# Attention's loads spread between products, w_out three slices ahead, conversions into buffers of their own

## The chip, the cores and the metric

One core of a Trainium2 chip runs the whole program. The metric is device time in microseconds (us) of one execution; lower is better. The engines are PE (TensorE, matmuls), DVE (VectorE), ACT (ScalarE), POOL (GpSimd) and SP (SyncE, which here does nothing but start DMA transfers). Each engine works through its own list of instructions in program order. A DMA is started by an instruction on an engine's queue: SPq is SP's, ACTq is ScalarE's.

## What is computed

```python
# attention in chunks of 64 along the sequence (q, k, v: 8 x 8 x 576 x 64)
scores = scale * np.matmul(q_c, k_c.transpose(0, 1, 2, 4, 3))
scores = scores - np.max(scores, axis=-1, keepdims=True)
attn = np.exp(scores)
attn = attn / (np.sum(attn, axis=-1, keepdims=True) + 1e-09)
out = np.matmul(attn, v_c)
x = np.ascontiguousarray(attn_out.transpose(0, 2, 1, 3)).reshape(B * S, H * D)   # 4608 x 512
# phase 0, d_ff 1536
x = ((x @ w_a) * (x @ w_b)) @ w_out
# phase 1, d_ff 1024
h = ((x @ w1) * (x @ w2)) @ w3
return h @ w_out2
```

## The kernel before

The 4608 tokens are nine blocks of 512. A block's attention comes in four **units** (two heads each); a unit loads q and k (`load1`) and v (`load2`) from memory with many small DMAs, turns them (`turn`), and goes on with `scores`, `soft1`, `soft2`, `flip`, `apply`, `put`. These pieces are laid by a planner, `Track`, between the matmul products of the block before: at every `point()` between products it emits pieces in step with their planned costs. `load1` and `load2` start all DMAs of their unit in a row on SP's queue: in blocks of full-length runs 16 for q and k, 12 for v.

Values are split into a high and a low part (`split`: a cast on ACT, a subtraction on POOL or DVE), and a product is three passes of matmuls over these parts.

A phase begins with **plain steps** (block 0 and part of block 1, `plain_step`), during which the weights are converted; then come **Strassen blocks** of two token blocks each (`strassen_step`, 12 steps in phase 0, 8 in phase 1; seven products P1 to P7 per step), and last the **lone block** (the ninth, at half width). The second factor's product, g times w_out, is done slice by slice (`Second`, four parts of three matmuls) one step behind. For the other token block of a pair it is done in a **burst** between two Strassen blocks: `burst` runs all slices in a row, 12 or 8, after the first of which the pending slice of the last step is finished. For each slice it needs `wo` (512 KB of w_out, loaded on SP's queue, four buffers, two slices ahead) and `gh`, `gl` (the two parts of g, made by `g_parts` on ACT and POOL, three buffers). During a burst the next block's attention begins: `attention_begins` starts the loads of its first two units before the first slice. During the steps of the first Strassen block of a phase, sums of weights (`su`, loaded two steps ahead) are formed on DVE and `w` tiles are loaded on SP's queue when a product has set their buffer free (`load_part`).

The weights arrive as float32 and are converted by `Conv`, driven by `Pump`: `load` (a DMA of 512 KB into a raw tile `cv`), `s1` (DVE, ACT), `s2` (three operations on DVE, then one addition on POOL which writes the result over a third of the raw tile), and a `sink` that casts the result on ACT and subtracts on DVE or POOL one job later. In the lone block of phase 0 this is done for w_out2 (jobs `o2`) and w3 (`w3`, two per row block; each is turned by PE in `turn_w3` two jobs later, and `fuse` multiplies it by w_out2), with three raw buffers (`G2`, `xo1`, `xo2`). The result stays in the raw tile until its last reader is done; only then can the next load go into that buffer.

`tick()` stands ahead of every product and every part of a slice; it sends off waiting stores on ACT's queue. On SP's queue everything goes out in program order, and an instruction that waits for a buffer holds all behind it.

## Time and profile before

| | |
|---|---|
| median of 3 runs | 1890.5 us (1886.52 to 1900.22) |
| the profiled execution | 1885.44 us, span 1883.6 us |
| mean granted TensorE clock in it | 0.937 of full speed |
| busy: PE | 1621.7 us, 86% of the span |
| busy: DVE, ACT, POOL | 882.9, 558.7, 442.2 us |
| DMA | 385.45 MB, 291704 packets |

Busy time of PE is that of pipelined matmuls, whose ends are modelled; a busy PE is not PE at its peak. The share is an average over stages that have different limits, so the stages are looked at one by one. In the timeline, each row gives the start, the duration, the engine, the line of the kernel, the operation with output and inputs, a count, and in brackets how long the engine had been idle and what ended that.

### The profile page before, as it was taken

The page shows a single profiled execution, that of the slowest core. Times are in us where ns is not written, and L with a number is a line of the kernel's source. Part 1 is how long each engine was busy: PE and PEld are TensorE (multiplying, and loading weights), DVE is VectorE, ACT ScalarE, POOL GpSimd, SP SyncE. Part 2 cuts the span into 40 slices and gives each one's busy share as a digit, 9 for nine tenths or more (in the row PEclk, how much of TensorE's full clock was granted, in tenths as well). Part 3 has the DMA queues.
Part 4 walks back from the last instruction along what each step waited for, and adds up shares of the span by engine and source line. Part 5 has one row for each costly group of instructions (what it writes and reads, how often), then busy time and mean ns, then how long its engine had stood idle before and what let it go on. Part 6 is the DMA issues. An engine that isn't in the chain of part 4 may idle for free.

```text
span 1883.6 us, 24887 instructions
## 1 busy us (share of the span) xinstructions
PE 1621.7 (86%) x9232; PEld 1308.6 (69%) x9232; DVE 882.9 (47%) x1484; ACT 558.7 (30%) x1009; POOL 442.2 (23%) x354
## 2 busy tenths in 40 slices
PE   5679994999876999699998577789989989989998
PEld 3567783777655787477877466677867867868787
DVE  5667662576652555445324443346554442242231
ACT  4444442322232222232223221223233232142232
POOL 1323331211121121221223221123221221222222
PEclk7879997999998999899999789899999999999999
DMA  7657754666755666666566565558647756656675
GB/s 194 226 169 238 248 196 110 215 198 217 234 160 175 189 190 212 178 214 196 179 193 220 186 223 189 168 200 317 234 149 270 260 178 219 212 184 205 192 271 176
DMA packets 291704, 385.45 MB, mean 205 GB/s; under 512 B 174848, under 2 KB 195328, under 8 KB 291584
## 3 DMA queue, kind: packets, MB, share of 16 engines
q1 hardware_dynamic: 259328, 299.97, 51.4%
q10 hardware_dynamic: 32256, 83.90, 11.5%
q8 instruction: 73, 1.20, 0.3%
q14 instruction: 47, 0.39, 0.1%
HBM read 301.99 MB, written 81.79 MB: 204 GB/s over the span
## 4 chain that ended last, share of the span: by engine, by line
PE 65%; DVE 9%; DMA 8%; SPq 6%; issue 5%; ACT 4%; POOL 3%; ACTq 1%; POOLq 0%; DVEq 0%
PE P L735 32%; PE acc L764 19%; PE pb L721 5%; PE pa L721 4%; PE wf L966 3%; SPq L278 2%; DMA cv_o<-in_moe_w_out_dram 2%; SPq L300 2%; DMA cv_w<-in_moe_w_dram 2%; DVE xP L539 1%; DVE xP L225 1%; PE x L371 1%; PE s L321 1%; DMA wo<-dwo 1%; DVE c L823 1%
## 5 line engine op out<-in xcount | busy, mean ns | idle before, releaser
L735 PE MATMUL P<-xP,w 128*128 128x512 f32 (+1 forms) x3360 | 741.1, 374 | 72.1 <-DVE c L823 30.7
L735 PEld LDWEIGHTS P<-xP,w 128*128 128x128 f32 x3360 | 592.0, 195 | 194.3 <-DVE c L823 40.1
L823 DVE TENSOR_TENSOR c<-P,c 128x512 f32<-128x512 f32 (+1 forms) x240 | 148.7, 622 | 338.6 <-PE P L735 330.7
L851 POOL TENSOR_TENSOR G<-c,c 128x512 f32<-128x512 f32 x60 | 77.9, 1299 | 514.5 <-DVE c L823 514.5
L820 ACT COPY c<-P 128x512 f32<-128x512 f32 (+1 forms) x240 | 127.1, 532 | 224.7 <-PE P L735 220.4
L764 PE MATMUL acc<-gh,wo 128*128 128x512 f32 x480 | 175.2, 403 | 0.0
L224 ACT CAST gh<-c 128x512 fp32r<-128x512 f32 x60 | 37.3, 621 | 326.1 <-DVE c L850 311.4
L721 PE MATMUL pa<-xq,w 128*128 128x512 f32 x480 | 123.0, 407 | 1.9 <-DVE w L624 1.9
L721 PE MATMUL pb<-xq,w 128*128 128x512 f32 x480 | 123.7, 409 | 0.0
L225 POOL TENSOR_TENSOR gl<-c,gh 128x512 fp32r<-128x512 f32 x60 | 77.9, 1298 | 159.9 <-ACT gh L224 159.9
L764 PE MATMUL acc<-wo,gh 128*128 128x512 f32 x320 | 111.1, 390 | 0.5 <-ACT gh L224 0.5
L721 PEld LDWEIGHTS pa<-xq,w 128*128 128x128 f32 x480 | 92.5, 196 | 22.8 <-DVE w L624 2.3
L721 PEld LDWEIGHTS pb<-xq,w 128*128 128x128 f32 x480 | 93.4, 197 | 20.5 <-DVE w L624 0.2
L764 PEld LDWEIGHTS acc<-gh,wo 128*128 128x128 f32 x480 | 92.9, 194 | 19.8
L225 DVE TENSOR_TENSOR xP<-xP,xP 128x512 fp32r<-128x512 f32 (+1 forms) x64 | 52.4, 819 | 105.0 <-ACT xP L224 105.0
L850 DVE TENSOR_TENSOR c<-P,c 128x512 f32<-128x512 f32 x60 | 41.5, 691 | 119.2 <-PE P L735 119.2
L764 PE MATMUL acc<-gl,wo 128*128 128x512 f32 x240 | 96.0, 400 | 0.0
L179 POOL TENSOR_TENSOR cv<-cv 128x512 f32<-128x512 f32 x40 | 48.3, 1208 | 132.1 <-DVE cv L175 125.4
L225 DVE TENSOR_TENSOR xP<-x,xP 128x512 fp32r<-128x512 f32 (+1 forms) x48 | 45.9, 1002 | 55.1 <-ACT xP L224 55.0
L764 PEld LDWEIGHTS acc<-wo,gh 128*128 128x128 f32 x320 | 60.1, 188 | 13.4 <-ACT gh L224 1.0
L224 ACT CAST xP<-xP 128x512 fp32r<-128x512 f32 (+1 forms) x64 | 36.2, 565 | 103.1 <-DVE xP L539 103.1
L764 PE MATMUL acc<-wo,gl 128*128 128x512 f32 x160 | 62.8, 393 | 0.9 <-POOL gl L225 0.8
(128 smaller groups left out, 2158.8 us busy)
## 6 DMA issues: line engine op xcount, KB each, us to landing
w<-dw SPq DMA_DIRECT2D x200, 512.0 KB, 4.3
wo<-dwo SPq DMA_DIRECT2D x168, 512.0 KB, 4.3
dw<-w ACTq DMA_DIRECT2D x80, 512.0 KB, 3.8
w<-dw SPq DMA_DIRECT2D x80, 256.0 KB, 3.3
d<-cv ACTq DMA_DIRECT2D x40, 256.0 KB, 4.4
su<-d SPq DMA_DIRECT2D x20, 512.0 KB, 5.5
cv_o<-in_moe_w_out_dram SPq DMA_DIRECT2D x19, 512.0 KB, 5.9
x2d<-ev ACTq DMA_DIRECT2D x36, 256.0 KB, 3.0
```

The source lines that it names most:

```text
L179: eng.tensor_tensor(self.w, hi.bitcast(F32), lo, op=ALU.add)
L224: nc.scalar.copy(dst_h, src)
L225: eng_l.tensor_tensor(dst_l, src, dst_h, op=ALU.subtract)
L278: nc.sync.dma_start(tv[g : g + 32, off // 32 : (off + n) // 32, :], src[b, 2 * self.hp + h, s : s + n, 32 * e : 32 * e + 32].rearrange("(t ...
L721: nc.tensor.matmul(ps, w[m][:, kk // 2, wp, kk % 2], xq[kk // 2][:, kk % 2, xp], start=(n == 0), stop=(n == 3 * KM - 1),)
L735: nc.tensor.matmul(ps, w[:, wp, kt], x[:, kt, xp], start=(begins and n == 0), stop=(n == 5), skip_group_check=True,)
L764: nc.tensor.matmul(acc[m], a, b, start=(f == 0 and (wp, gp) == SEQ[0]), stop=(f == NF[ph] - 1 and (wp, gp) == SEQ[-1]),)
L820: nc.scalar.copy(t, src)
L823: add = lambda o, a, b: nc.vector.tensor_tensor(o, a, b, op=ALU.add)
L850: nc.vector.tensor_tensor(g, last, c11, op=ALU.mult)
L851: nc.gpsimd.tensor_tensor(g_place(ph, nm.split("_")[0], f, gplaces), c22, c12, op=ALU.mult)
L966: nc.tensor.matmul(ps, t[:, gp, jj], wo2[jj // 2][:, jj % 2, wp], start=(jj == 0 and (wp, gp) == SEQ[0]), stop=(jj == NF[1] - 1 and (wp, g ...
```

## The change

Five things are changed.

1. Attention's loads are no longer started where `load1` and `load2` stand. `ask` puts them in a list; `tick` sends off two ahead of each product and one ahead of each part of a slice, eight per round in the opening. `settle` sends off what is left of a unit's loads where they are first needed (`turn` for q and k, `sums` for v).
2. In a burst `wo` is asked for three slices ahead instead of two, the first three ahead of the new attention loads' sending.
3. The parts `gh`, `gl` of a burst's first slice are made ahead of the last step that precedes the burst; `gh` and `gl` have four buffers instead of three, `tmp` five instead of six.
4. In the lone block the conversion's last addition writes into a tile of its own (`cw`, four buffers that attention used before), and the next raw tile is asked for right behind every conversion, as far as three ahead.
5. In the opening, three raw weight loads move from SP's queue (and one from the first instruction of ACT's) to ACT's queue, one in each of the first three rounds; the raw loads that stood in later rounds go out from the first plain steps on.

```diff
-        return pool.tile([P, n], F32, tag="tmp", name=name, bufs=6)
+        return pool.tile([P, n], F32, tag="tmp", name=name, bufs=5)
...
+    def ask(to, src):
+        asks["left"].append((to, src))
+        asks["all"] += 1
+
+    def settle(n):
+        while asks["done"] < n and asks["left"]:
+            nc.sync.dma_start(*asks["left"].popleft())
+            asks["done"] += 1
+
-    def tick(every=False):
+    def tick(every=False, loads=0):
+        settle(asks["done"] + loads)
...
             self.w = b.bitcast(F32)
+            if self.out:
+                self.w = pool.tile([P, NT], F32, tag=self.out, name=f"cw_{self.nm}")
             eng.tensor_tensor(self.w, hi.bitcast(F32), lo, op=ALU.add)
...
                         for e in range(2):
                             g = 32 * (2 * h + e)
-                            nc.sync.dma_start(
+                            ask(
...
         def turn(self):
+            settle(self.qk_end)
...
     def product(ps, w, x, begins):
-        tick()
+        tick(loads=2)
...
             self.m += 1
-            tick()
+            tick(loads=1)
...
-        gh = pool.tile([P, NT], F32R, tag="gh", name=f"gh{nm}", bufs=3)
-        gl = pool.tile([P, NT], F32R, tag="gl", name=f"gl{nm}", bufs=3)
+        gh = pool.tile([P, NT], F32R, tag="gh", name=f"gh{nm}", bufs=4)
+        gl = pool.tile([P, NT], F32R, tag="gl", name=f"gl{nm}", bufs=4)
...
-        for f in range(2):
-            ready(f)
+        parts = [ready(ph, j, 0, gplaces) if first is None else first]
+        parts.append(ready(ph, j, 1, gplaces))
+        state["outs"].ahead(3)
...
+            state["outs"].ahead(3)
...
-            return dict(tag=["G2", "xo1", "xo2"][n % 3])
+            return dict(tag=["G2", "xo1", "xo2"][n % 3], out=["qk0", "qk1", "ep0", "ep1"][n % 4])
...
                 pump.run()
-                if kind:
+                while pump.loaded < min(pump.cap, pump.done + 3):
                     pump.load(slot(kind))
...
-        for i in range(4):
+        for i in range(3):
             pump.load(slot("Y"), nc.scalar)
...
-                if t > 1:
-                    pump.load(slot("Y"))
-            tick()
+            if t < 3:
+                pump.load(slot("Y"), nc.scalar)
+            tick(loads=8)
...
+                if f + 1 == n and not single:
+                    state["ready"] = ready(ph, j + 1, 0, gplaces)
...
-                            track.append((1.0, True, lambda ic=turns[n_ - 2]: turned(ic)))
+                            track.append((1.0, True, lambda ic=turns[n_ - 2]: turn_w3(*ic)))
...
-                            track.append(conv_piece(None))
+                            track.append(conv_piece("G"))
```

What the change does to the engines' lists is seen at three places. The first is SP's list at the first burst of phase 0 (`qk` and `v` are attention loads, `wo` the slices of w_out). Before, from the second unit's 28 loads on (the first unit's 28 stand ahead of them):

```order
L278 DMA qk_1_3005<-in_q_dram 32x8x32 x8
L278 DMA qk_1_3005<-in_k_dram 32x8x32 x8
L300 DMA v_1_3022<-in_v_dram 64x2x64 x2
L300 DMA v_1_3022<-in_v_dram 64x64
L305 DMA v_1_3022<-in_v_dram 64x64
L300 DMA v_1_3022<-in_v_dram 64x64
L305 DMA v_1_3022<-in_v_dram 64x64
L300 DMA v_1_3022<-in_v_dram 64x2x64 x4
L659 DMA wo_2_3041<-dwo_2_166 128x1024
L659 DMA wo_3_3100<-dwo_3_167 128x1024
L659 DMA wo_4_3126<-dwo_4_168 128x1024
```

And in the changed kernel:

```order
L680 DMA wo_2_2989<-dwo_2_166 128x1024
L148 DMA qk_0_2981<-in_q_dram 32x8x32 x8
L680 DMA wo_3_3052<-dwo_3_167 128x1024
L148 DMA qk_0_2981<-in_k_dram 32x8x32 x4
L680 DMA wo_4_3082<-dwo_4_168 128x1024
L148 DMA qk_0_2981<-in_k_dram 32x8x32 x4
L680 DMA wo_5_3111<-dwo_5_169 128x1024
L148 DMA v_0_2982<-in_v_dram 64x2x64 x2
L148 DMA v_0_2982<-in_v_dram 64x64 x2
L680 DMA wo_6_3142<-dwo_6_170 128x1024
```

All 56 small loads stood ahead of the third slice's `wo`; now eight stand behind it and four between two slices, for as long as there are any. The second place is POOL's list at the end of the same Strassen block (`gl_3b` are low parts for the burst behind it, `G` and `gl_11` belong to the block's last step). Before:

```order
L851 TENSOR_TENSOR G_2_4672<-c_11_4999,c_11_5032 128x512
L225 TENSOR_TENSOR gl_11_5096<-c_11_5012,gh_11_5095 128x512
L225 TENSOR_TENSOR gl_3b_5156<-G_0_3477,gh_3b_5155 128x512
L225 TENSOR_TENSOR gl_3b_5160<-G_0_3477,gh_3b_5159 128x512
L225 TENSOR_TENSOR gl_3b_5215<-G_0_3477,gh_3b_5214 128x512
```

And in the changed kernel:

```order
L241 TENSOR_TENSOR gl_10_4987<-c_10_4865,gh_10_4986 128x512
L241 TENSOR_TENSOR gl_3b_4991<-G_0_3471,gh_3b_4990 128x512
L872 TENSOR_TENSOR G_2_4671<-c_11_5003,c_11_5036 128x512
L241 TENSOR_TENSOR gl_11_5100<-c_11_5016,gh_11_5099 128x512
L241 TENSOR_TENSOR gl_3b_5108<-G_0_3471,gh_3b_5107 128x512
```

One low part of the burst has moved ahead of the last step's two operations; its cast has done the same on ACT. The third place is POOL's list at the start of the lone block of phase 0 (`cv` are raw tiles, `cw` the new ones). Before:

```order
L179 TENSOR_TENSOR cv_o_0_8987<-cv_o_0_8987 128x512
L179 TENSOR_TENSOR cv_o_1_8989<-cv_o_1_8989 128x512
L179 TENSOR_TENSOR cv_o_2_8991<-cv_o_2_8991 128x512
L847 TENSOR_TENSOR g_0_9089<-c_0_9002,c_0_9050 128x256
L225 TENSOR_TENSOR gl_0_9093<-g_0_9089,gh_0_9092 128x512
```

And in the changed kernel:

```order
L195 TENSOR_TENSOR cw_o_0_9011<-cv_o_0_8989 128x512
L195 TENSOR_TENSOR cw_o_1_9041<-cv_o_1_8991 128x512
L195 TENSOR_TENSOR cw_o_2_9069<-cv_o_2_8993 128x512
L868 TENSOR_TENSOR g_0_9092<-c_0_9002,c_0_9052 128x256
L241 TENSOR_TENSOR gl_0_9096<-g_0_9092,gh_0_9095 128x512
```

Nothing has moved here; the addition's target is another tile, so that it is the raw tile's last reader. On PE's list no instruction has moved anywhere, and on DVE's only the first operation of one conversion, in the first plain step.

## Rows read from the trace of the kernel before

**Rows 1.** The page's head: the span of the profiled execution.

```profile
span 1883.6 us, 24887 instructions
```

**Rows 2.** Stretches: length, busy us of PE, PEld, DVE, ACT, POOL, PEclk, DMA, GB/s.

```profile
291.34:361.40 70.06, 39.59 (x157) 31.55 (x158) 27.48 (x35) 18.26 (x33) 14.64 (x11) 0.78 0.54 161
361.40:542.30 180.90, 165.93 (x1148) 129.71 (x1147) 118.94 (x229) 50.45 (x95) 29.95 (x23) 0.97 0.69 217
542.30:609.39 67.09, 39.08 (x156) 31.53 (x157) 23.55 (x25) 18.76 (x33) 17.99 (x13) 0.80 0.49 143
...
772.47:830.68 58.21, 40.97 (x158) 32.96 (x158) 23.54 (x25) 18.77 (x33) 17.98 (x13) 0.82 0.57 166
...
986.52:1028.20 41.68, 37.94 (x156) 30.50 (x157) 16.79 (x23) 15.79 (x33) 17.19 (x13) 0.96 0.63 201
1028.20:1266.11 237.91, 171.00 (x893) 146.93 (x892) 100.34 (x191) 57.83 (x113) 52.98 (x49) 0.86 0.57 195
...
1379.58:1417.82 38.24, 28.92 (x110) 21.28 (x110) 23.26 (x33) 15.96 (x28) 9.28 (x7) 0.96 0.61 208
...
1515.20:1552.87 37.67, 30.45 (x109) 22.13 (x110) 20.58 (x23) 16.39 (x29) 12.39 (x9) 0.91 0.51 171
...
1650.25:1686.46 36.21, 28.97 (x109) 21.28 (x110) 20.58 (x23) 16.39 (x29) 12.41 (x9) 0.95 0.54 176
```

**Rows 3.** Timeline of PE in the first burst.

```profile
327.99 0.76 PE L764 MATMUL acc<-gh_1b,wo 128*128 128x512 f32 x1 [27.32 <-DMA wo<-dwo]
...
342.96 0.61 PE L764 MATMUL acc<-gh_1b,wo 128*128 128x512 f32 x2
...
343.64 0.61 PE L764 MATMUL acc<-gh_1b,wo 128*128 128x512 f32 x2
```

**Rows 4.** Waits of PE: who waited for whom, us in total, times, longest.

```profile
PE acc L764 <- DMA wo<-dwo: 66.8, 3, 27.3
```

**Rows 5.** Timeline of SP's queue in the first burst.

```profile
291.74 5.24 SPq L278 DMA_DIRECT2D qk<-in_q_dram  x8
...
323.35 20.35 SPq L659 DMA_DIRECT2D wo<-dwo  x9
```

**Rows 6.** Timeline of PE at the start of the second burst.

```profile
543.57 0.51 PE L764 MATMUL acc<-gh_3b,wo 128*128 128x512 f32 x1 [1.27 <-ACT gh_3b L224]
545.68 0.50 PE L764 MATMUL acc<-gl_3b,wo 128*128 128x512 f32 x1 [1.61 <-POOL gl_3b L225]
```

**Rows 7.** Timeline of the lone block: third conversion, and the tenth's addition.

```profile
1037.12 0.33 SPq L159 DMA_DIRECT2D cv_o<-in_moe_w_out_dram  x1
...
1041.22 0.43 DVE L165 TENSOR_SCALAR cv_o<-cv_o 128x512 int32<-128x512 int32 x1 [3.79 <-DMA cv_o<-in_moe_w_out_dram]
...
1043.57 1.36 POOL L179 TENSOR_TENSOR cv_o<-cv_o 128x512 f32<-128x512 f32 x1 [5.58 <-issue]
...
1044.42 4.66 PE L735 MATMUL P<-xP,w 128*128 128x256 f32 x24 [7.52 <-DVE c L823]
...
1092.83 1.04 POOL L179 TENSOR_TENSOR cv_w<-cv_w 128x512 f32<-128x512 f32 x1 [2.16 <-DVE cv_w L175]
```

**Rows 8.** Timeline: a `fuse`, the last w3 addition; chain: products of phase 1's lone block.

```profile
1130.68 5.79 PE L966 MATMUL wf<-wo,w3t 128*128 128x512 f32 x24 [0.69 <-DVE w3t L225]
...
1229.11 1.04 POOL L179 TENSOR_TENSOR cv_w<-cv_w 128x512 f32<-128x512 f32 x1 [2.01 <-PE P L735]
...
1827.79 4.31 PE P L735 x36
```

**Rows 9.** Timeline of the opening: a raw weight load and who waits for it.

```profile
43.76 0.64 SPq L159 DMA_DIRECT2D cv_o<-in_moe_w_out_dram  x1
...
50.84 0.43 DVE L165 TENSOR_SCALAR cv_o<-cv_o 128x512 int32<-128x512 int32 x1 [6.39 <-DMA cv_o<-in_moe_w_out_dram]
```

**Rows 10.** Timeline of the first Strassen block: loads ahead of `su`, and PE.

```profile
445.11 3.90 SPq L278 DMA_DIRECT2D qk<-in_k_dram  x8
...
455.84 1.13 PE L321 MATMUL s<-kT,qT 64*64 64x64 f32 x32 [4.26 <-DVE c L823]
```

More of the change, by code (lines that the diff above doesn't have):

```diff
@@ L137, in store @@
         stores.append([0, to, src])
-    def tick(every=False):
+    asks = {"left": deque(), "all": 0, "done": 0}
+    def ask(to, src):
[7 more added lines that the diff above has]
+        settle(asks["done"] + loads)
         for s in stores:
@@ L154, in load @@
         def load(self, slot, queue=None):
+            self.out = slot.pop("out", None)
             t = pool.tile([P, 3 * NT], I32, name=f"cv_{self.nm}", **slot)
@@ L265, in load1 @@
             self.load_qk()
+            self.qk_end = asks["all"]
         def load2(self):
@@ L269, in load2 @@
             self.load_v()
+            self.v_end = asks["all"]
         def load_qk(self):
@@ L299, in every_other @@
             if whole:
-                nc.sync.dma_start(
+                ask(
                     to[:, c0 : c0 + whole, :],
@@ L304, in every_other @@
             for c in range(whole, cnt):
-                nc.sync.dma_start(to[:, c0 + c, :], hs[s0 + c * P : s0 + c * P + CH, :])
+                ask(to[:, c0 + c, :], hs[s0 + c * P : s0 + c * P + CH, :])
         def turn(self):
+            settle(self.qk_end)
             self.t = [self.work("qT"), self.work("kT")]
@@ L365, in sums @@
         def sums(self, place):
+            settle(self.v_end)
             self.x = self.banks("x")
@@ L410, in load_qk @@
                     for h in range(2):
-                        nc.sync.dma_start(
+                        ask(
                             to[:, :, h],
@@ L423, in load_v @@
                     if off % P == 0 and n % P == 0:
-                        nc.sync.dma_start(
+                        ask(
                             tv[:, off // P : (off + n) // P, h, :],
@@ L436, in turn @@
         def turn(self):
+            settle(self.qk_end)
             self.t = [self.work("qT"), self.work("kT")]
@@ L730, in product @@
     def product(ps, w, x, begins):
-        tick()
+        tick(loads=2)
         n = 0
@@ L880, in plain_step, with ready, burst @@
         point()
-    def burst(ph, j, gplaces, others):
+    def ready(ph, j, f, gplaces):
+        return g_parts(gplaces[f // 4][:, f % 4], f"{ph}_{j}b{f}", nc.gpsimd)
+    def burst(ph, j, gplaces, others, first=None):
         n = NF[ph]
-        sums, parts = [], []
+        sums = []
         track = Track(others, 2 * n // 3)
-        def ready(f):
-            parts.append(g_parts(gplaces[f // 4][:, f % 4], f"{ph}_{j}b{f}", nc.gpsimd))
-        for f in range(2):
-            ready(f)
+        parts = [ready(ph, j, 0, gplaces) if first is None else first]
+        parts.append(ready(ph, j, 1, gplaces))
+        state["outs"].ahead(3)
         for f in range(n):
             if f and f + 2 < n:
-                ready(f + 2)
+                parts.append(ready(ph, j, f + 2, gplaces))
             s = Second(ph, j, f, state["outs"].next(), parts[f], sums, ("rC", "rA", "rB", "rD"))
@@ L902, in burst @@
                 state["pending"].rest()
-                ready(2)
+                parts.append(ready(ph, j, 2, gplaces))
+            state["outs"].ahead(3)
         track.finish()
@@ L1014, in chunk_attention_two_gated_products @@
         U = [First(T, hp, T) for T in range(2) for hp in range(NHP)]
-        for i in range(4):
+        for i in range(3):
             pump.load(slot("Y"), nc.scalar)
-        for u in U[:2]:
+        for u in U[:NHP]:
             u.load1()
             u.load2()
-        for u in U[2:4]:
-            u.load1()
-            u.load2()
+        settle(asks["all"])
         plain = {0: [], 1: []}
@@ L1055, in chunk_attention_two_gated_products @@
                 pump.run()
-                if t > 1:
-                    pump.load(slot("Y"))
-            tick()
+            if t < 3:
+                pump.load(slot("Y"), nc.scalar)
+            tick(loads=8)
         units = unit_list(1)
@@ L1075, in point @@
                 (at or late).point(pe)
+            if n + 1 == len(order):
+                state["ready"] = ready(0, 1, 0, plain[0])
             plain_step(0, 0, T, f, f"0_{T}_{f}", point, plain[0], sums[0], "AC")
@@ L1155, in point @@
                         nxt.point(pe)
+                    if n_ + 1 == len(order):
+                        state["ready"] = ready(1, 1, 0, plain[1])
                     plain_step(1, 0, T, f, f"1_{T}_{f}", point, plain[1], sums[1], "AC" if T else "BD")
@@ L1178, in chunk_attention_two_gated_products @@
                     attention_begins(units)
-                burst(ph, j + 1, places, pieces)
+                burst(ph, j + 1, places, pieces, state.pop("ready", None))
                 steps = NF[ph]
@@ L1192, in chunk_attention_two_gated_products @@
                     track = [conv_piece("G") for i in range(NF[1])]
-                    def turned(ic):
-                        turn_w3(*ic)
-                        pump.load(slot("G"))
                     turns = [(i, c) for i in range(NF[1]) for c in range(2)]
```

## The prediction

> **What bounds it now.** The prediction is made against the profiled execution: 1885.4 us, of which the span is 1883.6 [rows 1]. I first cut the span by stage with the table of stretches, then asked in each slow stage what the Tensor engine (PE) waits for (the list of waits), and last read the timeline there. Where PE is not the bound, two things show. Rows 2 give eight bursts and the lone block. A burst of phase 0 is 13 slices (12 of its own, one pending) of 12 matmuls; three matmuls start 0.68 us after the three before [rows 3], so a slice needs 2.72 us and the burst 35.4 us. It takes 70.1, 67.1, 58.2 and 41.7 us. A burst of phase 1 has 9 slices, 24.5 us; the first three take 38.2, 37.7 and 36.2 us [rows 2]. The lone block takes 237.9 us at a mean granted clock of 0.86. The block of steps between the first two bursts runs at 0.97 [rows 2], so far less is to be had there.
>
> In the bursts the list of waits names one releaser: PE waits for `wo<-dwo`, 66.8 us in 3 times [rows 4]. The timeline shows why: SyncE's queue (SPq) begins with the attention loads of two units at 291.74 and reaches the next `wo` only at 323.35; that is 56 loads in 31.6 us, 0.565 us each [rows 5]. PE restarts at 327.99, 4.6 us after the issue, at 0.76 us for a matmul that otherwise shows 0.39 [rows 3]: the granted clock of this burst is 0.78, so part of it ran at 1.2 GHz instead of 2.4. The fourth burst has no attention loads, and none of this.
>
> **The bursts' loads.** The rows of the order show `wo` first, then 8 loads, then `wo` after every four. Each part of a slice lets one load go, so SPq has 4 x 0.565 and some 0.33 for a large load (as one takes in rows 7), 2.6 us of issuing per slice of 2.72. With three slices ahead, slice 3 is asked for when the pending slice ends and is needed 5.4 us later, against the 4.6 us from issue to use of rows 3 and 5: a slack of about 0.8 us. If a load costs 5.24/8 = 0.66 us, as the first eight do [rows 5], SPq needs 2.97 us per slice and falls 0.25 x 12 = 3 us behind; I take 2 us lost per burst. So bursts 1 to 3 should look like the fourth, 41.7 us.
>
> **The first slice's parts.** Every burst behind a Strassen block starts with PE waiting for the Scalar engine's `gh` (1.27 us) and GpSimd's `gl` (1.61 us) [rows 6]: 2.9 us, six times. After, both stand ahead of the last step in program order and lie under it, one cast and one subtraction in a step whose products keep PE busy; without that cover they cost the same 2.9. With 41.7 - 2.9 + 2 (loads) - 0.8 I take 40 us for bursts 1 to 3 and 38.5 for the fourth. In phase 1 the fourth `gh`/`gl` buffer lets the cast run one slice further ahead of PE; nothing of before shows how much of the remaining excess this takes, bounds being none of it and all. I take about half for the two behind a block: 37.7 and 36.2 become 31 and 30; the first, behind plain steps, goes from 38.2 to 35; the last loses its start, about 3. The gains are 30 + 27 + 18 + 3 + 3 + 7 + 6 + 3 = **97 us** (bounds 60 and 120).
>
> **The lone block.** With three buffers a conversion goes round thus: Vector waits 3.79 us for the load, works from 1041.22, GpSimd's addition ends at 1044.93, the next load starts when the previous job's low part is done [rows 7]. The conversions come 49.3/7 = 7.04 us apart, from the addition at 1043.57 to that at 1092.83, eight additions. The load takes 4.1 us (issued at 1037.12, used at 1041.22), so it was issued 2.9 us after the last conversion began: 2.9 + 4.1 = 7.0, the period. PE's adds stand behind it in Vector's queue, and PE waits 7.52 us at 1044.42. After, the raw buffer is free once the addition has ended, 3.7 us after the start, and the load then issued is wanted two conversions later: 3.7 + 0.1 + 4.1 = 7.9 us for two, 3.9 each, still above the 3.2 us that Vector works on one with its add (1041.22 to PE's restart at 1044.42). I take 4.1: (7.04 - 4.1) x 7 = 20.6 us. Against it stands 2.7: the burst's third slice ahead makes SPq wait one slice longer before it comes to the block's first load.
>
> Then come w3's pairs: from 1092.83 to 1229.11 seven pairs, 19.5 us each [rows 7, 8]. A step of the lone block has 42 products' matmuls, 36 of which take 4.31 us in phase 1, and 12 of w_out [rows 8, 3]: 5.0 + 2.7 = 7.7 us. By its share of the pieces' planned cost a pair stands over 0.96 of a step, and adds `fuse` (24 matmuls at 0.227 = 5.4 us) and two transposes (0.7): 13.5 us for PE. Today a load's wait falls inside, because the raw buffer is held until the transpose two jobs on. After it is not, but the short waits for Vector around `fuse` (0.69 us before it at 1130.68) stay, some more per pair: between 13.5 and 19.5 I take 16 us, 3.5 x 7 = 24. The lone block gives 20.6 - 2.7 + 24 = **42 us** (bounds 15 and 75).
>
> **The rest.** (a) Opening: `cv_o` is issued at 43.76, behind the second block's v loads, and Vector waits 6.39 us for it [rows 9]. After it is asked for on the Scalar engine's queue two rounds earlier: 6 us (2 to 10; the three issues there hold Scalar some 0.6 us each, as SPq's 0.64, 1.9 in all). The Trainium skill's page "DMA: Bandwidth & Descriptors", section "Issuing engines are not separate DMA queues", says another issuing engine saves only issue time. By that the sum would be 5.4 us less; here it is the place in the order that moves. (b) Block 1: 16 q/k loads go out in a row, `su` behind the last 3.90 us of them, and PE stands 4.26 us at 455.84 behind Vector, which waits for `su` [rows 10]; its clock of 0.97 over 181 us [rows 2] is some 5 us more. Spread at most 18 per step (7 products x 2 + 4), they leave `su` in time: 10 us (0 to 15). (c) The plain steps: 4 us (0 to 8). (d) Five instead of six `tmp` buffers: a step takes three or four, so the buffer wanted is one whose last reader stands most of a step earlier in program order, in steps of 7.7 us and more: nothing. That cover gone, a GpSimd operation of 1.36 us [rows 7] would be waited for, at most 1.4 us per step.
>
> Sum: 97 + 42 + 6 + 10 + 4 = 159; 1885.4 - 159 = 1726. The runs' median is 5 us above the profiled execution, their lowest 1 above; I put **1728 us**.
>
> **Rivals.** *The loads choke the queue.* If each attention load holds SPq for twice 0.565 us once they lie between `wo` loads, a slice lasts 4 x 1.13 + 0.33 = 4.85 instead of 2.72 us, 25 us per burst: 1728 + 75 = 1803. For it speaks that 0.66 was seen; against it that a `wo` right behind 56 of them was used after 4.6 us, no backlog. The skill's same page, "Specifications", puts line rate at 512 bytes and up, while q/k rows here are 128 bytes; that is this rival's ground, and no run shows it in a burst so far.
> *The lone block keeps its pace.* If, with the loads away, Vector's and Scalar's queues still pace a conversion at 6.5 us and a pair at 19, its gain is 5: 1728 + 37 = 1765. For it: the waits for `c` adds are many and short; against: the 7.0 is explained by the load alone.
> *Slower: the trickled q/k come late to `turn`.* `turn` first sends off all loads of its unit that are still queued; had none gone before, 16 x 0.565 = 9 us plus some 2 us of landing would hold Vector with PE's adds behind it, in each of the 20 units of blocks 1 to 3: 220 us, 1728 + 220 = 1948. It passes 1885 from 7.9 us per unit. Against it: no `wo` in the new order has more than 18 loads before it, so none is sent in a rush.
> *It doesn't do what it says:* SPq enters the bursts late, because it waits for the last products' `w` buffers. That is today's case already, and `wo` of slices 0 to 2 goes out ahead of the loads.
>
> **Numbers.** As summed, 0.74; choked loads 0.08; lone block unchanged 0.13; slower 0.04; nothing moves 0.01. The range 1685 to 1790 takes in the terms' bounds (bursts 120 and lone block 62 give 1685, bursts 60 and lone block 17 give 1790) and the lone-block rival. Faster by over 1% 0.95, within 1% 0.01, slower by over 1% 0.04; 1% is about what a measurement of this kernel can tell from no change.
>
> **What would show it.** Waits of PE for `wo` near 0 to 6 us in all; bursts of phase 0 at 38 to 42 us, and no 1.27/1.61 at their start; conversions' additions 4 us apart, pairs 16; no 6.39 us at 50; block 1 at some 171 us instead of 181. Wrong would be: a slice period above 3 us in a burst, Vector's waits for `cv` still over 3 us each, or `turn` waiting for q/k.

## The result, and the profile after

The changed kernel takes 1787.5 us (median of 4 runs, 1784.7 to 1791.1) against 1893.6 us for the kernel before beside it: a ratio of 0.944, 95% interval 0.940 to 0.948. The profiled execution took 1786.45 us, against the 1885.4 us on which the sum was made: 99 us less. The forecast was 1728 us, 159 less. So the direction was right, the time lies at the upper end of the range (1790), and 60 us of the gain did not come.

The page's head:

```profile
span 1784.6 us, 24867 instructions
```

The table of stretches (same columns as [rows 2]) for, in this order, burst 1, block 1, bursts 2 and 3, the lone block, the plain steps of phase 1, and the first two bursts of phase 1:

```profile
292.46:345.65 53.19, 40.02 (x157) 30.45 (x157) 27.95 (x35) 18.17 (x32) 13.92 (x10) 0.90 0.65 185
345.65:530.76 185.11, 168.18 (x1150) 130.43 (x1149) 120.68 (x228) 51.20 (x96) 31.30 (x24) 0.97 0.71 220
530.76:571.55 40.79, 37.47 (x157) 28.80 (x156) 24.28 (x25) 17.86 (x32) 16.80 (x12) 1.00 0.78 214
...
734.98:777.16 42.18, 37.95 (x158) 30.18 (x156) 24.27 (x25) 17.86 (x32) 16.79 (x12) 0.96 0.80 228
...
971.04:1166.07 195.03, 157.24 (x894) 135.74 (x893) 103.75 (x191) 57.37 (x113) 53.30 (x49) 0.94 0.68 240
1166.07:1284.33 118.26, 112.98 (x481) 91.66 (x479) 59.55 (x89) 36.09 (x63) 30.27 (x25) 0.97 0.67 239
1284.33:1322.27 37.94, 29.70 (x109) 21.70 (x109) 23.09 (x33) 15.97 (x28) 8.22 (x6) 0.91 0.56 190
...
1420.15:1455.03 34.88, 29.09 (x110) 22.14 (x109) 20.34 (x23) 15.77 (x28) 11.20 (x8) 0.90 0.58 185
```

Set against [rows 2], and with the stretches that are not shown, the 99 us are made up like this (gain in us; minus is a loss):

| stage | before | after | gain | forecast |
|---|---|---|---|---|
| opening and plain steps, phase 0 | 291.3 | 292.5 | -1.1 | 10 |
| burst 1 | 70.1 | 53.2 | 16.9 | 30 |
| block 1 | 180.9 | 185.1 | -4.2 | 10 |
| burst 2 | 67.1 | 40.8 | 26.3 | 27 |
| burst 3 | 58.2 | 42.2 | 16.0 | 18 |
| burst 4 | 41.7 | 37.6 | 4.1 | 3 |
| lone block, phase 0 | 237.9 | 195.0 | 42.9 | 42 |
| plain steps, phase 1 | 113.5 | 118.3 | -4.8 | 0 |
| four bursts, phase 1 | 141.9 | 136.3 | 5.6 | 19 |
| all other blocks | 681.0 | 683.7 | -2.7 | 0 |

As totals, bursts 2 to 4 and the lone block came close to the sum. Four places did not: burst 1, block 1, the opening with its plain steps, and the bursts of phase 1.

**Burst 1.** The 66.8 us of [rows 4] have become 11.6, of which one wait is 8.8. From the list of waits of the whole run, then the timeline of burst 1 (SP's queue, one store on Scalar's queue, PE), then SP's longest wait between 293 and 346 us:

```profile
PE acc L785 <- DMA wo<-dwo: 11.6, 4, 8.8
```

```profile
318.82 0.34 SPq L680 DMA_DIRECT2D wo<-dwo  x1
...
328.55 0.93 ACTq L157 DMA_DIRECT2D dw<-w  x2
...
331.20 1.11 SPq L148 DMA_DIRECT2D qk<-in_q_dram  x2
...
333.42 0.40 SPq L680 DMA_DIRECT2D wo<-dwo  x1
...
337.92 0.76 PE L785 MATMUL acc<-gh_1b,wo 128*128 128x512 f32 x1 [8.85 <-DMA wo<-dwo]
```

```profile
SPq L148 <- DMA dw<-w: 12.2, 2, 12.0
```

SP's queue does not run behind: it stands still, from 319.2 to 331.2 us, ahead of a small q load, and goes on 2.65 us after a *store* was issued on another queue. The program says why. Landings of transfers are counted on eight counters, which the transfers of SP's and Scalar's queues take in turn, in program order; a transfer waits until the one before it on its counter has landed. In the built program this holds for all 1456 transfers. It names the same counter, DMAHW6, for the store on Scalar's queue and for that load on SP's, the next transfer on it:

```
L157 DMA dw0_0_2_66<-w0_0_1_3244 128x1024 [waits DMAHW6_49,DVE_49]
L148 DMA qk4_1_2983<-in_q_dram 32x8x32 [waits DMAHW6_49]
```

The store waits for Scalar's cast and Vector's subtraction of a weight sum, these for Vector's sums, and Vector was busy with the next block's operands until 324.9. Before the change all 56 loads went out ahead of these stores in program order; spread out, they come behind them.

**Block 1** shows the same. SP's waits for the landing of `dw<-w` and Vector's waits for loads there, from 345 to 531 us:

```profile
SPq L148 <- DMA dw<-w: 19.1, 9, 6.0
...
SPq L692 <- DMA dw<-w: 4.8, 4, 1.5
```

```profile
DVE kT L329 <- DMA qk<-in_k_dram: 9.1, 3, 3.8
DVE qT L328 <- DMA qk<-in_q_dram: 2.7, 1, 2.7
DVE kT L329 <- DMA w<-dw: 1.2, 1, 1.2
```

Before, SP waited 10.4 us for these stores in that block, and Vector waited for `su` [rows 10], not for q or k.

**Plain steps.** PE now waits at `turn`, and SP from 100 to 292 us waits longer for the stores of converted weights than before (27.7 us, 5 times):

```profile
123.19 1.08 PE L462 MATMUL t<-ident,qk 128*128 128x128 f32 x4 [4.72 <-DMA dwo<-wo]
125.29 1.08 PE L462 MATMUL t<-ident,qk 128*128 128x128 f32 x4 [1.01 <-DMA qk<-in_k_dram]
...
216.82 1.09 PE L462 MATMUL t<-ident,qk 128*128 128x128 f32 x4 [2.81 <-DMA v<-in_v_dram]
```

```profile
SPq L173 <- DMA d<-cv: 57.4, 9, 16.6
```

A raw weight load stands at the head of SP's queue until the store out of its buffer has landed, and the trickled q and k, which before had gone out ahead of it, stand behind it.

**Phase 1's bursts.** In the first of them the cast of one `gh` (1305.06) and the next (1312.09) are seven us apart:

```profile
1305.06 0.61 ACT L240 CAST gh_1b<-G1p 128x512 fp32r<-128x512 f32 x1
...
1305.76 1.27 POOL L241 TENSOR_TENSOR gl_1b<-G1p,gh_1b 128x512 fp32r<-128x512 f32 x1 [3.00 <-ACT gh_1b L240]
1305.80 1.77 DVE L560 TENSOR_TENSOR xP<-x,x 128x512 f32<-128x512 f32 x1
...
1307.60 0.62 ACT L240 CAST xP<-xP 128x512 fp32r<-128x512 f32 x1 [1.93 <-DVE xP L560]
...
1309.58 0.62 ACT L240 CAST xP<-xP 128x512 fp32r<-128x512 f32 x1 [1.36 <-DVE xP L560]
...
1311.56 0.62 ACT L240 CAST xP<-xP 128x512 fp32r<-128x512 f32 x1 [1.36 <-DVE xP L560]
1312.09 0.61 ACT L240 CAST gh_1b<-G1p 128x512 fp32r<-128x512 f32 x1
...
1312.75 0.80 PE L785 MATMUL acc<-wo,gh_1b 128*128 128x512 f32 x1 [2.84 <-ACT gh_1b L240]
```

Three casts of `xP`, the next block's operands, stand between them in Scalar's queue, each waiting for Vector. A further buffer for `gh` does not change that.

**The lone block.** Vector's waits for raw tiles from the third conversion on, before (1035 to 1215 us) and after (980 to 1160):

```profile
DVE cv_w L165 <- DMA cv_w<-in_moe_w_dram: 30.8, 9, 4.9
DVE cv_o L165 <- DMA cv_o<-in_moe_w_out_dram: 13.6, 5, 3.8
```

```profile
DVE cv_w L179 <- DMA cv_w<-in_moe_w_dram: 2.4, 1, 2.4
DVE cv_o L179 <- DMA cv_o<-in_moe_w_out_dram: 1.2, 2, 0.7
```

The wait that the sum was to remove is nearly gone. How far the two terms of the sum came is read at the run "w3 asked late".

### The profile page after: what moved, and what is told of

Same layout as the page of the kernel before. It is cut to its first block, busy times and chain, and to the rows that moved or that the text cites. A ratio compares the mean times of both kernels' runs of the same rounds, so it can differ in the third digit from the quotient of the medians.

```text
span 1784.6 us, 24867 instructions
## 1 busy us (share of the span) xinstructions
PE 1609.8 (90%) x9232; PEld 1293.8 (72%) x9232; DVE 888.5 (50%) x1484; ACT 557.4 (31%) x1009; POOL 442.7 (25%) x354
## 4 chain that ended last, share of the span: by engine, by line
PE 62%; DVE 14%; DMA 8%; issue 5%; ACT 5%; POOL 2%; SPq 2%; ACTq 1%; POOLq 0%; DVEq 0%
PE P L756 32%; PE acc L785 16%; PE pb L742 5%; PE pa L742 4%; PE wf L988 3%; DVE xP L560 2%; SPq L148 2%; DVE xP L241 2%; DMA wo<-dwo 1%; DVE c L844 1%; ACT xP L240 1%; PE x L391 1%; DMA qk<-in_k_dram 1%; DMA x2d<-ev 1%; ACT ev L794 1%
## 5 line engine op out<-in xcount | busy, mean ns | idle before, releaser
L756 PEld LDWEIGHTS P<-xP,w 128*128 128x128 f32 x3360 | 584.3, 192 | 177.5 <-DVE c L844 40.9
L785 PEld LDWEIGHTS acc<-wo,gh 128*128 128x128 f32 x320 | 60.5, 189 | 16.9 <-ACT gh L240 4.1
L241 DVE TENSOR_TENSOR xP<-x,xP 128x512 fp32r<-128x512 f32 (+1 forms) x48 | 49.7, 1080 | 40.7 <-ACT xP L240 40.7
L241 DVE TENSOR_TENSOR xP<-xP,xP 128x512 fp32r<-128x512 f32 (+1 forms) x64 | 44.2, 691 | 43.8 <-ACT xP L240 43.8
```

The lines of the kernel that those rows point to most:

```text
L241: eng_l.tensor_tensor(dst_l, src, dst_h, op=ALU.subtract)
L756: nc.tensor.matmul(ps, w[:, wp, kt], x[:, kt, xp], start=(begins and n == 0), stop=(n == 5), skip_group_check=True,)
L785: nc.tensor.matmul(acc[m], a, b, start=(f == 0 and (wp, gp) == SEQ[0]), stop=(f == NF[ph] - 1 and (wp, gp) == SEQ[-1]),)
```

## The experiments

Each starts from the changed kernel. "Stage" is a length cut at the same places of the program as above (some cuts differ by up to 0.2 us from the table); ratios are to the kernel before, run on the same chip.

| run | median us | ratio, 95% interval | stage that it speaks of |
|---|---|---|---|
| changed kernel | 1787.5 | 0.944 (0.940 to 0.948) | |
| stores held in bursts | 1790.8 | 0.948 (0.944 to 0.951) | burst 1 53.2 to 43.2; block 1 185.3 to 189.4 |
| loads at once, plain steps | 1779.8 | 0.942 (0.938 to 0.946) | plain 292.5 to 284.3 |
| loads at once, block 1 | 1789.6 | 0.947 (0.943 to 0.951) | block 1 to 189.9 |
| two slices ready | 1783.1 | 0.944 (0.941 to 0.948) | starts of bursts, below |
| pieces spread | 1760.5 | 0.931 (0.929 to 0.933) | burst 1 to 42.6; phase 1's four, 135.8 to 120.7 |
| older stores | 1789.0 | 0.946 (0.943 to 0.948) | block 1 to 188.3 |
| w3 asked late | 1801.9 | 0.953 (0.950 to 0.955) | lone block 195.0 to 210.0 |
| plain at once + two slices | 1771.8 | 0.937 (0.933 to 0.942) | |
| those two + pieces spread | 1748.9 | 0.925 (0.923 to 0.927) | block 1 188.6 |
| + `su` early, loads at once | 1745.9 | 0.923 (0.921 to 0.926) | block 1 184.7 |
| + `su` early, four loads a product | 1746.4 | 0.924 (0.922 to 0.926) | block 1 184.6 |
| sums not stored | 1775.1 | 0.938 (0.936 to 0.941) | block 1 185.3 to 175.3 |

### Stores held in bursts

```diff
-        while stores and (every or stores[0][0] > 1):
+        while stores and not asks["hold"] and (every or stores[0][0] > 1):
...
         state["outs"].ahead(3)
+        asks["hold"] = True
...
         track.finish()
+        asks["hold"] = False
```

> The changed kernel, but no store of a converted weight is issued inside a burst; those that fall due wait until it ends. Nothing is left out of the computation. Theory A (a late store stops SyncE's queue): in burst 1 SyncE stood from 319.2 to 331.2 because its next load may only be issued once an earlier transfer, the store dw<-w on the Scalar queue, has landed, and that store left only at 328.6. With the stores out of the way this standstill and PE's wait of 8.85 us for wo go; burst 1 from 53.2 to 42-45 us, the total 8 to 11 us less (ratio to the changed kernel about 0.995). Rival B (trickled loads are simply too many for the queue between two wo): SyncE still falls behind, burst 1 stays at 51 us or more, total within 2 us.

Burst 1, and block 1 behind it:

```profile
296.51:339.74 43.23, 38.18 (x157) 28.87 (x157) 30.12 (x35) 18.06 (x32) 14.01 (x10) 1.00 0.77 210
339.74:529.13 189.39, 170.93 (x1150) 132.37 (x1149) 120.94 (x229) 51.18 (x96) 31.24 (x24) 0.95 0.73 219
```

Theory A holds for the burst: without a store between them the same loads, at the same places, cost it nothing, and the granted clock rises from 0.90 to 1.00. The total did not move: the stores go out at the block's start, PE stands 3.2 us there behind a copy on Scalar, and block 1 and the first block of phase 1 take 4 us more each. (The opening also came out 4 us longer; that stage lies between 290.8 and 296.5 us in the seven experiments and the changed kernel that share it, so differences below 5 us say nothing there. Block 1 lies between 185.3 and 188.6 us in the changed kernel and the six experiments that leave its loads and stores alone.)

### Loads at once in the plain steps

```diff
     def ask(to, src):
         asks["left"].append((to, src))
         asks["all"] += 1
+        if asks.get("now"):
+            settle(asks["all"])
...
+        asks["now"] = True
         U = [First(T, hp, T) for T in range(2) for hp in range(NHP)]
...
         PTS = 7
+        asks["now"] = False
```

The last two assignments stand at the start of the opening and ahead of the first burst.

> The changed kernel, but up to the first burst every attention load goes out where it is asked for, as in the kernel before; bursts and blocks still take them one or two at a time. Theory C (in the plain steps the trickle makes turn late): PE's waits at turn of 4.72, 1.02, 2.81 and 2.36 us go, the stage up to burst 1 falls from 292.5 to 283-286 us, total 7 to 9 us less. Rival D (the loads in a row take the time elsewhere, by pushing raw weights and w_out back): the stage stays above 290 us, total within 2 us.

```profile
0.00:284.26 284.26, 232.98 (x1924) 184.88 (x1924) 185.34 (x335) 123.98 (x207) 82.60 (x68) 0.90 0.69 212
```

```profile
SPq L175 <- DMA d<-cv: 27.3, 5, 8.2
```

The waits at `turn` are gone, SP's wait for the stores is back at its value before (27.3 us), and the stage is 8.2 us shorter. The five kernels with this edit lie at 281.3 to 284.9 us, below all eight others. Theory C holds. Against the kernel before the stage now gains 7 us. The traces show where: the sixth unit's `turn` comes 9 us earlier in the changed kernel. Before, and in the changed kernel:

```profile
63.22 1.04 PE L441 MATMUL t<-ident,qk 128*128 128x128 f32 x8
```

```profile
54.10 1.04 PE L462 MATMUL t<-ident,qk 128*128 128x128 f32 x8
```

In all twelve experiments it stands between 55.3 and 56.6 us, with the trickle or without. At the ninth unit's `turn`, 117.42 us before, 5.4 us of the lead are left in this run and 6.3 in the changed kernel. So the opening gave some 5 to 7 us, and the trickle behind it took them back.

### Loads at once in block 1

```diff
+                if ph == 0 and sb == 1:
+                    settle(asks["all"])
+                    asks["now"] = True
                 j, places = block_steps(ph, sb, x, at)
+                asks["now"] = False
```

`ask` reads `now` as in the run above.

> The changed kernel, but inside the first Strassen block the attention loads go out where they are asked for; what the burst left over goes out ahead of the block. Theory E (the trickle traded Vector's wait for su against its wait for k): the waits of kT for in_k (3.4, 3.8, 2.0, 1.2 us) go and two waits for su of 7 to 9 us come back, block 1 falls from 185.1 to 180-182 us, total 3 to 5 us less. Rival F (the block is slow for another reason, the order of the loads does not matter): block 1 stays at 184-187 us.

```profile
DVE su L719 <- DMA su<-d: 26.5, 5, 10.2
```

The exchange of waits is as theory E says, k for `su`, but the price is not: block 1 takes 189.9 us, 4.6 more than in the changed kernel and 1.3 above the longest of the kernels that leave it alone. So the trickle inside this block is not what made it slower than before. E falls, and F's 184 to 187 us are missed too; whether the trickle helps there is hardly clear of the spread.

### Two slices ready

```diff
-        parts = [ready(ph, j, 0, gplaces) if first is None else first]
-        parts.append(ready(ph, j, 1, gplaces))
+        parts = first
...
-                    state["ready"] = ready(ph, j + 1, 0, gplaces)
+                    state["ready"] = [ready(ph, j + 1, i, gplaces) for i in range(2)]
```

> The changed kernel, but the high and low parts of the first two slices of a burst, not of the first alone, are made ahead of the last step before it. Theory G (the start wait moved from the first slice to the second, because the second's cast stands behind the casts of the last step's own product): the waits at the start of the bursts behind blocks (1.42+0.85, 1.50+0.85, 0.73+0.85, 2.23+0.85, 2.12+0.86, 1.10+0.86 us, 14.2 in all) go, total 10 to 14 us less. Rival H (Scalar and GpSimd are simply behind at that place, and the wait moves on to the third slice): total 0 to 3 us less, with waits of 1 to 2 us at the third slice.

The first `gh` and `gl` that PE waits for in burst 2, in the changed kernel and here:

```profile
535.85 0.58 ACT L794 COPY ev<-acc 128x512 f32<-128x512 f32 x1
...
539.84 1.14 ACT L240 CAST gh_3b<-G 128x512 fp32r<-128x512 f32 x2 [0.40 <-ACT ev L794]
540.51 0.50 PE L785 MATMUL acc<-gh_3b,wo 128*128 128x512 f32 x1 [1.43 <-ACT gh_3b L240]
541.86 0.50 PE L785 MATMUL acc<-gl_3b,wo 128*128 128x512 f32 x1 [0.85 <-POOL gl_3b L241]
```

```profile
542.39 0.50 PE L785 MATMUL acc<-gh_3b,wo 128*128 128x512 f32 x1 [0.31 <-ACT gh_3b L240]
543.74 0.50 PE L785 MATMUL acc<-gl_3b,wo 128*128 128x512 f32 x1 [0.84 <-POOL gl_3b L241]
```

By the order of the program these belong to the third slice, not to the second as the expectation has it: 36 matmuls go before them in the burst, twelve each of the first slice, the pending slice and the second. The second slice is in time in the changed kernel already. The third slice's cast stands in Scalar's queue behind four copies (`ev`, the first at 535.85) of the sums that the pending slice finishes. So theory G's ground is wrong. The edit takes one cast and one subtraction out of the burst's start, by which the first of these copies comes 3.8 us behind the start instead of 4.9.

The ratio does not move, and the median is 4.4 us lower, of 10 to 14 expected; by stages 1.4 us went in phase 1's second burst and 2.5 in its last. In the bursts of phase 0 behind blocks 3.8 of 6.2 us of waits for `gh` and `gl` are left, and waits for `wo` grow by 1 to 2 us in two of them. This is nearer to rival H: Scalar is behind at that place, and a second slice made ahead cures little of it.

### Pieces spread over the whole burst

```diff
-        track = Track(others, 2 * n // 3)
+        track = Track(others, n)
```

> The changed kernel, but the pieces that a burst takes in (the block's operands xP) are spread over all its slices instead of the first two thirds. Theory I (in phase 1 PE waits for gh and gl because their casts stand in Scalar's queue behind casts of xP that wait for Vector, and the pieces crowd together, so a fourth buffer could not help): the bursts of phase 1 fall from 37.9, 34.7 and 34.6 us to some 35, 32 and 32, those of phase 0 by about 1 us, total 6 to 12 us less. Rival J (the pieces are then late for the block's first step): bursts fall, the blocks behind them grow by as much, total within 2 us.

Burst 1 and the second burst of phase 1:

```profile
293.27:335.87 42.60, 37.33 (x157) 28.69 (x157) 26.46 (x29) 18.36 (x33) 14.29 (x10) 1.00 0.78 210
...
1407.05:1437.10 30.05, 26.39 (x109) 20.84 (x108) 19.51 (x21) 14.48 (x26) 11.69 (x8) 0.94 0.64 210
```

One number gives 27 us by the medians (22.5 between the two profiled executions), more than theory I asked for. The four bursts of phase 1 lose 15.1 us; the blocks behind the first three pay back 4.7 (J, but small). And burst 1 loses 10.6, of which block 1 pays back 3.2: the weight sums are the last pieces of its list, so their stores now come when its loads are out. SP does not wait for `dw<-w` in it at all.

### Older stores

```diff
-        while stores and (every or stores[0][0] > 1):
+        while stores and (every or stores[0][0] > 8):
```

> The changed kernel, but a store of a converted weight goes out after eight further products or parts of slices instead of after one. Theory L (loads that now stand between stores wait for stores that wait on the Scalar queue for Vector): SyncE's waits for the landing of dw<-w in block 1 fall from 23.9 us to under 10, the waits of kT for in_k go, block 1 from 185.3 to 178-181 us, burst 1 from 53.2 to 44-48; total 10 to 15 us less. Rival M (SyncE is full with loads of 0.55 us, the waits for stores lie in its slack): block 1 stays above 183 us, total at most 6 us less, from burst 1 alone.

SP's waits for `dw<-w` in block 1 rise, to 31.8 us, from 23.9; the block takes 188.3 us, burst 1 50.9. Theory L's cure fails, though not its cause (last run): SP runs far ahead of Scalar in program order, so wherever the store stands, the loads behind it get there first. That last sentence is argued from the order, not measured by itself.

### w3 asked late

```diff
-                while pump.loaded < min(pump.cap, pump.done + 3):
+                while kind and pump.loaded < min(pump.cap, pump.done + 3):
...
+                    def turned(ic):
+                        turn_w3(*ic)
+                        pump.load(slot("G"))
...
-                            track.append((1.0, True, lambda ic=turns[n_ - 2]: turn_w3(*ic)))
+                            track.append((1.0, True, lambda ic=turns[n_ - 2]: turned(ic)))
...
-                            track.append(conv_piece("G"))
+                            track.append(conv_piece(None))
```

> The changed kernel, but in the lone block the raw w3 tiles are asked for behind the transposes, as in the kernel before; the converted tiles keep their own buffers, and w_o2's loads are asked for as in the changed kernel. Theory N (both halves of that part are needed for w3): the first additions stay 4.0 us apart, a pair of w3 goes back from 16.4 to some 19 us, total 18 to 22 us more. Rival O (the own buffers alone did it, the early ask costs and brings nothing): pairs stay at 16.4 us, total within 2 us.

The additions that [rows 7, 8] show for the kernel before (the third; the tenth, which is the second of w3; the last), in the changed kernel, and the tenth and the last here:

```profile
985.72 1.42 POOL L195 TENSOR_TENSOR cw_o<-cv_o 128x512 f32<-128x512 f32 x1 [2.28 <-DVE cv_o L189]
...
1020.08 1.04 POOL L195 TENSOR_TENSOR cw_w<-cv_w 128x512 f32<-128x512 f32 x1 [1.10 <-DVE cv_w L189]
...
1128.95 1.04 POOL L195 TENSOR_TENSOR cw_w<-cv_w 128x512 f32<-128x512 f32 x1 [2.01 <-PE P L756]
```

```profile
1022.40 1.04 POOL L195 TENSOR_TENSOR cw_w<-cv_w 128x512 f32<-128x512 f32 x1 [1.09 <-DVE cv_w L189]
...
1145.89 1.04 POOL L195 TENSOR_TENSOR cw_w<-cv_w 128x512 f32<-128x512 f32 x1 [2.01 <-PE P L756]
```

In the changed kernel a conversion takes (1020.08 - 985.72) / 7 = 4.91 us and a pair (1128.95 - 1020.08) / 7 = 15.6, against 7.04 and 19.5 before; asked late, a pair takes (1145.89 - 1022.40) / 7 = 17.6. (The 4.0 and 16.4 us of the expectation divide by seven from the ninth addition, at 1013.97, where there are six conversions and seven and a half pairs.) The total is 14.4 us longer, the block 15.0, less than the 18 to 22 expected. Theory N holds for w3: of the 3.9 us that a pair gains, the own buffer alone brings 1.8, and the early ask 2.1 more, 15 us in the block. For w_out2 this run does not tell the two halves apart. But there the kernel before already asked for the next tile right behind each conversion, so what the change altered was the buffer.

### The combinations

> The changed kernel with two of the changes above together: attention loads at once up to the first burst, and two slices made ahead of a burst. Theory: they lie in different stages and add up, 8 + 4 us: 1775 to 1777 us. Rival: what the plain steps gain is given back in burst 1 and block 1, where the loads of the next units start earlier in time but not in order: 1780 or more.

> The changed kernel with three of the edits tried before together: attention loads at once up to the first burst, two slices made ahead of a burst, the burst's pieces spread over all its slices. If they act in different places they add up: 26 + 8 + 4 less than 1787, some 1748 us (1744 to 1753). Rival: the slice made ahead and the spreading remove the same waits for gh and gl at a burst's start, so 3 to 4 us are lost again: 1753 to 1757.

Both add up: 1771.8 us (3 us below the expected range), then 1748.9. The three edits act in different places.

> As the three together, and in block 1 the attention loads go out where they are asked for, while each su is asked for one step earlier than before. Theory P (loads in a row are harmless in block 1 once su no longer stands behind them): the waits of Vector for su of 5.9, 7.5, 2.6 and 10.2 us, seen with the loads in a row, go; block 1 from 188 to 172-176 us, total 10 to 15 us below the three together. Rival Q (SyncE has no room left in that block; with su ahead, another load comes late, k or a weight): block 1 stays at 183 us or more.

> As the three together, su asked for one step earlier, and in block 1 up to four attention loads go out per product instead of two. Theory P: the waits for su do not arise and the waits of kT for in_k of 2 to 4 us go, since a unit's loads are out in half the time; block 1 at 172-178 us. Rival Q: SyncE still waits some 20 us for stores in that block, kT still waits for in_k: 183 us or more.

The edit for `su`, in both:

```diff
-                    if f + 2 < n:
-                        su[f + 2] = summed(ph, f + 2, f + 2)
-                        su[f + 2].load()
+                    if f + 3 < n:
+                        su[f + 3] = summed(ph, f + 3, f + 3)
+                        su[f + 3].load()
```

In both Vector no longer waits for `su`, and block 1 takes 184.7 and 184.6 us: rival Q. In the first SP waits 21.3 us for `dw<-w` and PE once stands 7.9 us for a weight tile; in the second SP's waits for `dw<-w` are 12.6 us. The totals, 1745.9 and 1746.4, are the best of all, but their intervals overlap that of the three edits alone.

### Sums not stored

```diff
-            nc.sync.dma_start(whole(t).bitcast(F32), dw[ph][f][0 if i == 0 else i + 1])
+            nc.sync.dma_start(whole(t).bitcast(F32), dw[ph][f if i == 0 or ph else 0][0 if i == 0 else i + 1])
...
-            store(dw[self.ph][self.f][2 + i], whole(t).bitcast(F32))
+            if self.ph or self.f == 0:
+                store(dw[self.ph][0 if self.ph == 0 else self.f][2 + i], whole(t).bitcast(F32))
```

> The changed kernel, but in phase 0 the weight sums are stored for the first slice alone (two stores, in burst 1); the 22 stores of block 1 are left out, and the later blocks read the first slice's sums in place of the others', so their numbers are not the reference's, while loads and products are as many as before. Theory L (SyncE's loads in block 1 wait for these stores): its waits for the landing of dw<-w, 23.9 us, go, the waits of kT for in_k (3.4, 3.8, 2.0, 1.2 us) shrink to under 3 us in all, block 1 from 185.3 to 172-178 us, total 8 to 13 us less. Rival M (SyncE is full with the loads themselves and PE's releases of the weight buffers): block 1 stays above 182 us, total within 3 us.

```profile
344.58:519.86 175.28, 168.01 (x1150) 130.78 (x1149) 122.22 (x229) 51.22 (x96) 31.23 (x24) 0.97 0.57 165
```

Block 1 loses 10 us, as theory L says. SP waits for no store of these there, and Vector for no q, k or `su`. Added up over SP's rows, with the pauses between loads of a row, a q load holds the queue for 0.52 us and a k load for 0.49, against 0.71 and 0.72 in the changed kernel; the issue itself takes nearly the same (0.47 and 0.44 us against 0.51 and 0.46). One doubt stays: the block also moves less (165 GB/s against 220), and Scalar is spared 22 issues; no run parts these from the waits, though the waits that went are those that name the store. And over the other runs the block's length does not follow SP's waits for stores: 12.6 us of them go with 184.6 us, 21.3 with 184.7, 31.8 with 188.3. So the stores as a whole cost 10 us here, but that they cost it through SP's queue is only in part shown.

## Why the prediction was half right

**Bursts 2 to 4** (46.4 us against 48): right, and by the reason given. `wo` ahead of the loads removes the stall of [rows 3 to 5]; the granted clock of burst 2 went from 0.80 to 1.00. Inside the sum two pieces offset each other: PE's waits for `wo` took 0.9 and 1.9 us of bursts 2 and 3, where 2 us each had been set for the loads, and PE's waits for `gh` and `gl` did not go but came to 2.3, 2.4 and 1.6 us, from 2.9 at each start.

**Burst 1** (16.9 against 30): the step that failed is the price of a load. The prediction charged each only its issue (2 us lost per burst) and did not ask what a load may have to wait for. It waited for a store on another queue, 12.0 us, and that made PE's 8.85. With the stores out of the burst it takes 43.2 us, with the pieces spread 42.6, against 40 forecast.

**The first slice's parts** (2.9 us, six times): the waits of [rows 6] went at the first slice, but most of them came back at the third: 1.43 and 0.85 us in burst 2. The claim that a cast and a subtraction lie under the step was right; what is late next, the third slice's cast behind the pending slice's copies on Scalar, was not named.

**The fourth buffer, phase 1** (with those starts, 5.6 against 19 for the four bursts): wrong cause. The term took half of an excess that it had not traced. The excess is Scalar's order: `gh` behind casts that wait for Vector. Spreading the pieces takes 15.1 us more from these bursts.

**The lone block** (42.9 against 42): right in its mechanism, the waits for raw tiles, but the total came by luck as well, because three misses cancel. A conversion took 4.91 us, not 4.1, so this term gave 14.9 us of 20.6. A pair took 15.6, not 16: 27.4 us, not 24. The 2.7 us set against it did not come: the third conversion's addition is 14.7 us behind the block's start, 15.4 before. The conversion's term held the load and Vector's own work alone; in the changed kernel additions 3.6 to 3.8 us apart alternate with ones 5.5 to 6.2 us apart, and in the first of these long gaps Vector stands 1.74 us for a product of PE (at 988.31). What else fills them was not traced.

**Opening and plain steps** (-1.1 against 10): the opening's part came, 5 to 7 us of the 6 forecast. On this term the Trainium skill was weighed, page "DMA: Bandwidth & Descriptors", section "Issuing engines are not separate DMA queues": only issue time saved would have meant 0.6 us. The gain speaks for the place in the order, which also moved; but no run here moves only the queue. The trickle's 4 us were of the wrong sign.

**Block 1** (-4.2 against 10): the step that failed is that spread loads leave `su` in time and nothing else comes late: waits for `su` became waits for k. The rows of [rows 10] were read rightly, the cure was not one: without the stores of weight sums, which SP's loads wait for, the block takes 10 us less.

**The rivals.** The slower one, that `turn` waits for trickled q and k, came true in small. It cost some 8 us in the plain steps and a share of block 1, not 220. Its dismissal ("no `wo` has more than 18 loads before it") looked at the wrong queue head: what stood ahead of q and k was a raw weight load and a store. The choked queue is refuted as it was put: bursts 2 and 3 take 40.8 and 42.2 us with the same trickle.

**Open.** Phase 1's plain steps took 118.3 us, and 113.9 to 118.0 in the experiments, against 113.5; a store's wait on Scalar's own queue (2.70 us ahead of `gh`) is part of it in the one trace, but no run tested it. The last 4 us of block 1 against before are not taken apart either; 3 us are the spread of that block between kernels that leave it alone.

## What to carry to other kernels

A load that is moved later in program order is moved behind the stores that stand there; where queues share counters of landings, such a store, with all that it waits for, can hold the load and everything behind it, so look up which store comes within eight transfers ahead. When an engine waits for a buffer's content, read the queue of the engine that fills it before adding buffers: here spreading a planner's pieces gave phase 1's bursts 15.1 us, where the fourth buffer and the early first slice together had given them 5.6.

## What the runs showed of the hardware

A subtraction of two SBUF tiles on Vector took 0.68 us alone and 1.77 us where GpSimd's subtraction of 1.27 us had begun 0.04 us ahead of it (the rows at 1305.76 and 1305.80): it ended 0.54 us after GpSimd had ended. Of the 48 such subtractions in the changed kernel's trace, the 27 with GpSimd idle took 0.68 to 0.69 us, the 21 beside a GpSimd operation 1.76 to 1.80. The Trainium skill, page "SBUF — State Buffer", section "SBUF: two separate sides", says that the port pair these two share is locked for a whole instruction and the other engine blocks; this trace agrees. So a `gl` that meets one of these costs Vector 1.1 us; that this is part of why the operands, and behind them `gh`, ran late is an inference.
